# A convolution-and-MLP kernel: the first filter spectrum in 4 KB rows, the second half's sums in other tables, and a new order of all instructions

## The chip, the cores and the metric

The kernel runs on one core of a Trainium2 chip. The metric is the device time of one execution in microseconds; the text gives medians. The core has five engines that run their own instruction lists and wait for one another by semaphores: TensorE (PE in the profile; PEld is its weight load), VectorE (DVE), ScalarE (ACT), GpSimd (POOL) and SyncE (SP), which here issues transfers and computes nothing. Sixteen DMA engines move the data.

## The reference

Four steps follow each other on x, 2048 rows of 512 bf16 numbers: a long convolution, an MLP, and both again.

```python
x = A_q
x = x + _A_ref(_layernorm(x), A_k, A_v, A_shift_k, A_ssm_k, A_ssm_D)
x = x + _B_ref(_layernorm(x), B_w1, B_b1, B_w2, B_b2)
x = x + _A_ref(_layernorm(x), A_k, A_v, A_shift_k, A_ssm_k, A_ssm_D)
x = x + _B_ref(_layernorm(x), B_w1, B_b1, B_w2, B_b2)
```

`_A_ref(q, k, v, ...)` shifts k by a filter of four taps along the rows, multiplies by v to get kv, convolves kv along the 2048 rows with a filter of 2048 taps for each of the 512 channels (by a Fourier transform of length 4096), adds kv times ssm_D, and returns q times the result. `_B_ref` is a layer norm, a 512 to 1376 matmul with bias and GELU, and a 1376 to 512 matmul with bias. The filter, k and v are the same in both convolutions, so the convolved result y is the same and is computed once.

## The kernel before, in words

**The convolution.** The 2048 rows are two halves of 1024, and so is the filter. A transform of one of these four pieces is two stages of matmuls: `stage1` (L584) against a table of cosines and sines, and `stage2` (L596) against a table of twiddles, in eight tiles t = 0 to 7. Every tile of 128x1024 is evacuated from PSUM to SBUF by ScalarE (L480) or VectorE (L481). The tags in the code are h for the filter, x for k-times-v, 1 and 2 for the stages, `_0` and `_1` for the halves.

The spectrum of the first filter half, `h2_0`, lands in `HH` (R_4). For a complex product the real and imaginary parts, which sit on even and odd partitions, must be had the other way round as well. So an exchange, `swap`, copies `HH` into `HI` (R_5) with even and odd partitions exchanged, in eight DMA transfers of 256 KB: two by t (0 to 3, 4 to 7), two by half of the channels, two by parity. Each moves 64 partitions. In `HH` the 64 numbers of one t stand 512 apart from one channel group to the next, so a source row is eight runs of 256 numbers (512 bytes).

The first half's output needs `x2_0` times `h2_0`. VectorE multiplies 128x1024 pieces from `HH` and `HI` (L475, tag `x2_0`, sixteen instructions) into R_1 and R_2; `inverse1` (L701) and `inverse2` (L723) transform back into y. The second half's output needs two products: `x2_0` with the spectrum h2_0 plus h2_1 terms (formed by L795 in R_3, exchanged into R_HS1, multiplied in place as tag `p2`), and `x2_1` with `h2_0`, which is multiplied in place in `HH` and `HI`. The second product is added to the first (tag `sum`), the sum stands in `HH` and `HI`, and the second `inverse1` reads it there.

Stage 2's table for t = 0 to 3 is built on the chip: one piece of 1024 columns (`tab_s`) is loaded into R_C, and eight scaled copies of it are spread (L525 on ScalarE, L526 on VectorE or GpSimd). R_C lies at the start of W1's place, so W1's first piece may be loaded when all eight are done. The first L596 needs all eight.

**The MLP.** The rows go through as blocks, 128 rows per tile: tiles of 1, 1, 2, 2, 2 and then 2, 2, 2, 2 in the first half, 4, 4 and 4, 4 in the second. A block takes statistics (L836, L837, L841 to L851), a normalised copy (L861, L862), the product with y and the sum (L475), statistics and normalised copy again, and a transposed copy, by TensorE for the first two blocks (L913), by a DMA transpose from SyncE for the others (L905). Then 11 chunks of the first layer (L925, GELU by L930) and the second layer (L959, added to x by L963). The first layer needs all four pieces of W1 (344 KB each), the second layer W2 (five pieces of 256 KB and a last one with the bias).

**The order.** Nothing is scheduled when the kernel is built. A table `SEQ` lists all 1187 operations in the order in which they are given to the engines' lists, `ENGS` gives the engine where there is a choice, and `BANKS` the PSUM bank of each tile. Each engine then runs its list in order, so an instruction that waits holds up all that stand behind it. `sync` derives the waits from what each operation reads and writes, and waits never change the order. The numbers of `dma` such as 690.0 are the durations by which the waits of one instruction are sorted; they take no part in the order. The transfers stand in SyncE's list, apart from four that ScalarE issues. The second half's k is loaded by DMA transposes (L511) into the place that the h1_1 matmuls read, so these come after those matmuls.

Of the kernel before, what the change touches and what calls it, by code (L numbers as in the profile page):

```python
# [7 lines left out]
ALU = mybir.AluOpType  # L8
# [28 lines left out]
class Prog:  # L37
# [65 lines left out]
            "vvvvavapvaaavvvvvvappavva")  # L103
    BANKS = (
            "60134220040246260464023527646260464422641704406260402044222460264036206002442040460240044204402200242060"
            "02214460672065547427762753146306163013472457323653454722637670216234677756017404705647420335536736732725"
            "64012131754124707451256025141142451241256076713424307574243075601201643645720014030")

    def __init__(self, nc):
# [289 lines left out]
def bass_interleave_layers__ssm_conv_h3__mixer_channel_mlp__prompt_kernel(  # L399
        nc, A_q, A_k, A_v, A_shift_k, A_ssm_k, A_ssm_D, B_x, B_w1, B_b1, B_w2, B_b2, out):  # L400
    P = Prog(nc)
# [598 lines left out]
```

## Time and profile before

| what | value |
|---|---|
| runs | 234.78, 235.28, 236.21 us; median 235.28 |
| the profiled execution, its own time | 236.31 us |
| its span, first to last instruction | 234.4 us |
| granted TensorE clock | 1.000 |
| busy: TensorE, VectorE, ScalarE, GpSimd | 224.6, 179.1, 167.0, 57.4 us |
| exchanges and their landing | 16 transfers of 256 KB, median 4.0 us |
| first matmul of the first layer | 57.07 us after the span's start |

All times in the text count from the start of the span. "A <-B" behind a wait names the instruction that ended it, by the latest semaphore that the profile saw; a matmul's end is modelled, so TensorE counts as busy while matmuls overlap. In the chain a line with L is work of that line and "DMA out<-in" a transfer under way. `ar` is the one SBUF arena in which every buffer lies, `ps` is PSUM and `sm` the small float32 arena, so rows tell buffers apart by line and shape only. `tab_small` holds the identity, the stage-1 table and constants, `tab_s` the stage-2 table, `in_B_w` W1 or W2.

### The profile page before, as it was taken

The numbers are of one execution on the slowest core, as the hardware profiler recorded it, in microseconds if no ns is written. First come the engines' busy times: TensorE is split into PE (matmuls) and PEld (weight loads), VectorE is DVE, ScalarE is ACT, GpSimd is POOL, SyncE is SP. The second block draws the span as 40 slices with busy tenths as digits, with TensorE's granted clock in tenths as the row PEclk, the third lists the DMA queues.
The fourth block names the chain that finished last, engine by engine and source line by source line (L and its number), as shares of the span: only waits on it lengthen the run. The fifth ranks groups of instructions, "written<-read, shape, count | busy, mean of one in ns | idle before, by whom it ended". The sixth has DMA issues, their size and how long they took to land.

```text
span 234.4 us, 6524 instructions
## 1 busy us (share of the span) xinstructions
PE 224.6 (96%) x2765; PEld 147.3 (63%) x2765; DVE 179.1 (76%) x360; ACT 167.0 (71%) x262; POOL 57.4 (24%) x119
## 2 busy tenths in 40 slices
PE   5999899997999999999999999999999999999995
PEld 1898787965868597667866585744444444444452
DVE  0699989999999999999999997771777769413023
ACT  2778999998969689999969996896077335603710
POOL 1496000207302525335003521312011010300000
PEclk9999999999999999999999999999999999999999
DMA  6999479479638970022400214232200310042102
GB/s 182 377 369 313 165 219 283 101 223 192 154 69 253 144 105 3 1 48 48 134 4 3 45 25 106 54 134 45 46 0 3 67 22 0 8 84 93 41 14 79
DMA packets 40105, 24.93 MB, mean 106 GB/s; under 512 B 23590, under 2 KB 33676, under 8 KB 40076
## 3 DMA queue, kind: packets, MB, share of 16 engines
q1 hardware_dynamic: 39778, 24.36, 39.7%
q8 instruction: 22, 0.36, 0.6%
q10 hardware_dynamic: 298, 0.16, 0.3%
q14 instruction: 7, 0.06, 0.1%
HBM read 13.23 MB, written 2.10 MB: 65 GB/s over the span
## 4 chain that ended last, share of the span: by engine, by line
PE 82%; ACT 8%; DMA 5%; DVE 2%; SPq 1%; issue 1%; ACTq 0%
PE ps L925 32%; PE ps L959 30%; ACT ar L480 7%; PE ps L584 5%; PE ps L701 4%; DMA ar<-ar 3%; PE ps L596 3%; DMA ar<-tab_small 2%; DVE ar L475 2%; PE ps L641 2%; PE ps L567 2%; PE ps L723 1%; SPq L460 1%; PE ps L948 1%; PE ps L669 1%; PE ps L616 1%
## 5 line engine op out<-in xcount | busy, mean ns | idle before, releaser
L930 ACT ACTIVATE ar<-ps,sm 128x256 bf16<-128x256 f32 (+5 forms) x143 | 66.8, 526 | 41.0 <-PE ps L925 40.3
L925 PE MATMUL ps<-ar 128*128 128x256 bf16 (+5 forms) x572 | 81.9, 297 | 1.2 <-ACT ar L861 1.0
L959 PE MATMUL ps<-ar 128*128 128x512 bf16 (+1 forms) x341 | 78.7, 379 | 0.0
L480 ACT ACTIVATE ar<-ps 128x1024 bf16<-128x1024 f32 (+3 forms) x76 | 70.3, 1022 | 7.0 <-PE ps L584 4.6
L925 PEld LDWEIGHTS ps<-ar 128*128 128x128 bf16 (+1 forms) x572 | 52.8, 100 | 28.5 <-ACT ar L861 1.1
L475 DVE TENSOR_TENSOR ar<-ar 128x512 bf16<-128x512 bf16 (+3 forms) x105 | 63.5, 641 | 1.0 <-ACT ar L480 0.3
L959 PEld LDWEIGHTS ps<-ar 128*128 128x128 bf16 (+1 forms) x341 | 32.5, 98 | 35.5 <-DVE ar L952 0.2
L836 DVE BATCH_NORM_STATS2 sm<-ar 128x6 f32<-128x512 bf16 x64 | 42.7, 682 | 0.7 <-DMA ar<-in_A_q_dram 0.2
L963 DVE TENSOR_TENSOR ar<-ar,ps 128x512 bf16<-128x512 bf16 x31 | 20.9, 681 | 18.4 <-PE ps L959 18.3
L861 ACT ACTIVATE ar<-ar,sm 128x512 bf16<-128x512 bf16 x39 | 30.6, 812 | 3.3 <-DVE sm L848 1.9
L841 POOL TENSOR_SCALAR sm<-sm 128x2 f32<-128x2 f32 (+2 forms) x21 | 6.1, 293 | 100.3 <-DVE sm L837 100.0
L843 POOL TENSOR_TENSOR sm<-sm 128x2 f32<-128x2 f32 (+2 forms) x26 | 22.0, 848 | 33.6 <-DVE sm L841 31.8
L584 PE MATMUL ps<-ar 128*64 128x128 bf16 x512 | 18.4, 225 | 1.0 <-issue 0.4
L596 PE MATMUL ps<-ar 128*128 128x64 bf16 x512 | 18.3, 193 | 0.9 <-ACT ar L480 0.8
L596 PEld LDWEIGHTS ps<-ar 128*128 128x128 bf16 x512 | 16.8, 98 | 2.7 <-ACT ar L480 1.8
L584 PEld LDWEIGHTS ps<-ar 128*64 128x64 bf16 x512 | 15.5, 112 | 4.0 <-ACT ar L480 1.8
L851 POOL TENSOR_SCALAR sm<-sm 128x1 f32<-128x1 f32 x40 | 14.8, 387 | 1.8
L481 DVE CAST ar<-ps 128x1024 bf16<-128x1024 f32 (+1 forms) x11 | 12.7, 1169 | 2.0 <-PE ps L584 0.8
L862 DVE TENSOR_SCALAR ar<-ar,sm 128x512 bf16<-128x512 bf16 x25 | 9.9, 411 | 5.1 <-POOL sm L851 5.0
L701 PEld LDWEIGHTS ps<-ar 64*128 64x128 bf16 (+1 forms) x384 | 11.8, 114 | 1.8 <-issue 0.4
L701 PE MATMUL ps<-ar 64*128 64x64 bf16 (+1 forms) x384 | 12.4, 203 | 0.2 <-DVE ar L475 0.2
L837 DVE BATCH_NORM_AGGREGATE sm<-sm 128x2 f32<-128x6 f32 x64 | 10.7, 174 | 0.8
(45 smaller groups left out, 100.8 us busy)
## 6 DMA issues: line engine op xcount, KB each, us to landing
ar<-ar SPq DMA_DIRECT2D x16, 256.0 KB, 4.0
ar<-tab_s SPq DMA_DIRECT2D x9, 256.0 KB, 5.0
ar<-in_A_ssm_k_dram SPq DMA_DIRECT2D x8, 256.0 KB, 5.2
ar<-in_A_v_dram SPq DMA_DIRECT2D x8, 256.0 KB, 5.3
ar<-in_A_q_dram SPq DMA_DIRECT2D x8, 256.0 KB, 4.7
out_dram<-ar SPq DMA_DIRECT2D x7, 256.0 KB, 2.8
ar<-in_B_w_dram SPq DMA_DIRECT2D x4, 344.0 KB, 5.7
ar<-in_B_w_dram SPq DMA_DIRECT2D x5, 256.0 KB, 3.8
```

The lines of the kernel that those rows point to most:

```text
L475: return P.op(eng, lambda e: e.tensor_tensor(o, a, b, op), dur, reads=[a, b] + list(more), writes=[o])
L480: return e.activation(dst, src(), AF.Copy)
L584: r = e.matmul(Q(tl, 64 * ri, 64, i * 128, [1, 128]), w, m, start=True, stop=True)
L596: r = e.matmul(Q(tl, 0, 128, i // 8 * 512 + i % 8 * 4, [32, 16], [1, 4]), w, m, start=True, stop=True)
L701: r = e.matmul(Q(tl, 0, 128, i, *([32, 16], [1, 4]) if split else ([1, 128],)), w, m, start=n == 0, stop=n == 1)
L836: P.op(DVE, lambda e, sj=sj, x=x: e.bn_stats(sj, x), 600.0, reads=[x], writes=[sj])
L843: P.op(POOL, lambda e: e.tensor_tensor(r, v, hf, ALU.pow), 420.0 + 149.0 * n, reads=[v, hf], writes=[r])
L861: return e.activation(o, x, AF.Identity, bias=u, scale=r)
L925: r = e.matmul(Q(tl, 0, rows, 0, [1, w]), a, m, start=dk == 0, stop=dk == 3)
L930: P.op(ACT, lambda e, dst=dst, tl=tl, rows=rows, bias=bias, w=w: e.activation(dst, Q(tl, 0, rows, 0, [1, w]), AF.Gelu_apprx_tanh, bias=bia ...
L959: r = e.matmul(Q(tl, 0, 128, 0, [1, 512]), ins[fc][0], ins[fc][1], start=fc == 0, stop=fc == 10)
L963: P.op(DVE, lambda e, x=x, tl=tl: e.tensor_tensor(x, x, Q(tl, 0, 128, 0, [1, 512]), ALU.add), 604.0, reads=[x], writes=[x], tile=tl)
```

## The change

Three things change. The spectrum `h2_0` gets a layout in which all that one transfer takes of a partition is one run of 2048 numbers (4 KB): `run(t)` puts t = 0 to 3 in the first 4096 columns and 4 to 7 in the second, with 256 numbers per channel group. The exchange of `h2_0` is written out with these runs; the second exchange keeps `swap`. `hrun` replaces `hap` wherever `HH` or `HI` is read. The sums go into R_3 and R_HS1, whose layout the second `inverse1` needs, and it reads them there. And `SEQ`, `ENGS` and `BANKS` are new.

```diff
-        8, 1, 4, 3, 0, 25, 33, 5, 46, 2, 35, 36, 29, 37, 30, 38, 40, 56, 47, 26, 6, 57, 50, 58, 48, 49, 216, 9, 32,
...
+        46, 35, 44, 5, 0, 36, 25, 47, 8, 56, 1, 37, 6, 50, 3, 48, 2, 12, 216, 49, 61, 62, 9, 11, 57, 51, 58, 38, 52,
...
+    def run(t):
+        return 4096 * (t // 4) + 64 * (t % 4)
+
+    def hrun(t, d, g=None):
+        return A(0, 128, HH + run(t) + (2048 * g if g else 0), [d, 2], [256, 16 if g is None else 8], [1, 64])
...
-        evac(BOTH, A(0, 128, HH + 64 * t, [32, 2], [512, 16], [1, 32]),
+        dst = A(0, 128, HH + run(t), [32, 2], [256, 16], [1, 32])
+        evac(BOTH, dst,
...
-    swap(HH, HI)
+    for kh in range(2):
+        for c in range(2):
+            for g in range(2):
+                o = 4096 * kh + 2048 * c
+                src, dst = [PA(p, r + o, [1, 2048]) for p, r in ((g, HH), (1 - g, HI))]
+                dma(dst, src, 1 << 18, reads=[src])
...
-            tt(hap(R_1, t, R_2 - R_1, g), A(0, 128, HX + 1024 * t + 512 * g, [0, 2], [64, 8], [1, 64]), hap(HH, t, HI - HH, g), ALU.mult, 603.0)
+            spec = hrun(t, HI - HH, g)
+            tt(hap(R_1, t, R_2 - R_1, g), A(0, 128, HX + 1024 * t + 512 * g, [0, 2], [64, 8], [1, 64]), spec, ALU.mult, 603.0)
...
-            o, x = A(0, 128, R_3 + w, [512, 16], [1, 32]), A(0, 128, HI + w, [512, 16], [1, 32])
+            o = A(0, 128, R_3 + w, [512, 16], [1, 32])
+            x = A(0, 128, HI + run(t) + 32 * g, [256, 16], [1, 32])
...
-        o, p = hap(HH, t, HI - HH), hap(R_3, t, D1)
+        o, p = hrun(t, HI - HH), hap(R_3, t, D1)
         tt(o, A(0, 128, xo, [0, 2], [64, 16], [1, 64]), o, ALU.mult, 1137.0)
         P.tag = "sum"
-        tt(o, o, p, ALU.add, 1137.0)
+        tt(p, o, p, ALU.add, 1137.0)
     P.tag = "i1_1"
-    inverse1(HH, HI, R_Z1, True)
+    inverse1(R_3, R_HS1, R_Z1, range(8))
```

`inverse1` now takes the set of tiles that are split by partition halves instead of a flag: none in the first inverse and all eight in the second, as before. A function `inverse1_by_half` is added and not called. The number of instructions of each kind stays; 49 of the 1187 operations go to another engine. In the changed file line numbers from L701 on are higher: L701 becomes L708, L723 L749, L836 L870, L905 L939, L913 L947, L925 L959 and L959 L993.

Three places in the engines' lists matter below. The first is SyncE's list behind the first exchange. `128x1376` is a piece of W1, `128x2x512` two rows of tiles of W2, `DMA_TRANSPOSE` with `in_A_k` a part of the second half's k. Before, from the exchange's last two transfers on:

```order
23 L460 DMA ar<-ar 64x8x256 x2
24 L460 DMA ar<-in_B_b_dram 1x512
25 L470 DMA ar<-tab_small 128x1024
26 L460 DMA ar<-in_B_w_dram 128x1376
27 L460 DMA ar<-in_B_b_dram 128x10x1
28 L460 DMA ar<-in_B_w_dram 128x1376
29 L460 DMA ar<-in_B_b_dram 96x1
30 L460 DMA ar<-in_B_w_dram 128x2x512 x2
31 L470 DMA ar<-tab_small 128x1024
32 L460 DMA ar<-in_B_w_dram 128x2x512
33 L460 DMA ar<-in_A_v_dram 128x1024
34 L511 DMA_TRANSPOSE ar<-in_A_k_dram 128x4x128
```

Row 35 behind these holds the last two pieces of W1. Now, from the same point on (the first piece of W1 stands further ahead):

```order
26 L460 DMA ar<-ar 64x2048 x2
27 L460 DMA ar<-in_A_q_dram 128x1024
28 L460 DMA ar<-in_B_w_dram 128x2x512
29 L470 DMA ar<-tab_small 128x1024 x2
30 L460 DMA ar<-in_B_w_dram 128x1376 x2
31 L460 DMA ar<-in_B_w_dram 96x512
32 L460 DMA ar<-in_B_w_dram 128x1376
33 L460 DMA ar<-in_B_w_dram 128x2x512
34 L460 DMA ar<-in_A_v_dram 128x1024
35 L511 DMA_TRANSPOSE ar<-in_A_k_dram 128x4x128
36 L460 DMA ar<-in_B_w_dram 128x2x512
```

All of W1 has moved ahead of v and of the transposed k. Two further loads of v, two further transposes of k and then the last W2 pair follow row 36, so that pair stands behind three transposes; before, all five W2 pairs stood ahead of the first one.

The second place is the head of ScalarE's list: its own transfers, the spreads (L525) and the first evacuations (L480). Before:

```order
1 L460 DMA ar<-in_A_shift_k_dram 4x512
2 L494 ACT_TABLE_LOAD
3 L470 DMA ar<-tab_small 128x464
4 L460 DMA ar<-in_A_ssm_D_dram 1x512
5 L525 ACTIVATE ar<-ar,sm 128x64x16 x3
6 L480 ACTIVATE ar<-ps 128x1024 x3
7 L480 ACTIVATE ar<-ps 128x8x128
```

Now:

```order
1 L470 DMA ar<-tab_small 128x464
2 L460 DMA ar<-in_A_shift_k_dram 4x512
3 L494 ACT_TABLE_LOAD
4 L460 DMA ar<-in_A_ssm_D_dram 1x512
5 L480 ACTIVATE ar<-ps 128x1024 x4
6 L480 ACTIVATE ar<-ps 128x8x128 x2
7 L525 ACTIVATE ar<-ar,sm 128x64x16 x2
8 L480 ACTIVATE ar<-ps 128x1024 x4
```

The small table goes out first, and two spreads stand behind six evacuations where three stood ahead of all.

The third place is the head of SyncE's list. Before:

```order
1 L460 DMA ar<-in_A_ssm_k_dram 128x1024
2 L470 DMA ar<-tab_s 128x1024
3 L460 DMA ar<-in_A_ssm_k_dram 128x1024 x2
4 L460 DMA ar<-in_A_k_dram 128x1024 x4
5 L460 DMA ar<-in_A_ssm_k_dram 128x1024
```

Now:

```order
1 L460 DMA ar<-in_A_ssm_k_dram 128x1024 x3
2 L460 DMA ar<-in_A_k_dram 128x1024 x4
3 L470 DMA ar<-tab_s 128x1024
4 L460 DMA ar<-in_A_ssm_k_dram 128x1024
5 L460 DMA ar<-in_A_v_dram 128x1024 x4
```

The piece of the stage-2 table from which the spreads copy was the second transfer and is now the eighth.

More of the change, by code (lines that the diff above doesn't have):

```diff
@@ L44 @@
     SEQ = (
[55 rows of a table removed]
[55 rows of a table added]
     ENGS = (
[L101 to L103 removed]
+            "vpvpvaavvvpvpvpvpaaavaavaavaavaavavvapvpvaaavavaavavvaaaaaaaaaavaaaaaaaaaavvavaaaappppaaaaaaaaaaaaaaaaaa"
+            "aaaaaaaaaaappvvvvappvppaappvvppaappaappaappaappaappaappvappaappaappaappvappaavpavpvaavvvvvavappavvvvpvav"
+            "vvvvvvvpvavaapvvavvppvava")
     BANKS = (
[L105 to L107 removed]
+            "43425704240260260464026421646260464422651146066240462042042460264073240000242624060240240420420402002660"
+            "04675406756463017126444564377357251031642372632034153077467642440510216372656247321154646670057122342670"
+            "61221570264135541541572503434012067362744465151532307422176457027100036327547357472")
     def __init__(self, nc):
@@ L459, in dma @@
     def dma(dst, src, nbytes, reads=(), writes=None, eng=SP, paced=False):
-        o = P.op(eng, lambda e: e.dma_start(dst, src, allow_slow_non_contiguous=True), 690.0 if P.tag[:2] == "h2" else 475.0, reads=reads,
+        o = P.op(eng, lambda e: e.dma_start(dst, src, allow_slow_non_contiguous=True), 690.0 if P.tag == "h2_1" or P.tag == "h2_0" and not 1 else 475.0, reads=reads,
                     writes=[dst] if writes is None else writes, dma=True, nbytes=nbytes)
@@ L679, in shift_pair, with inverse1 @@
                 P.op(DVE, g, 604.0, reads=[v], writes=[o], tile=tl[h])
+    def run(t):
+        return 4096 * (t // 4) + 64 * (t % 4)
+    def hrun(t, d, g=None):
+        return A(0, 128, HH + run(t) + (2048 * g if g else 0), [d, 2], [256, 16 if g is None else 8], [1, 64])
     def hap(r, t, d, g=None):
         return A(0, 128, r + 64 * t + (4096 * g if g else 0), [d, 2], [512, 16 if g is None else 8], [1, 64])
-    def inverse1(p, q, Z, split):
+    def inverse1(p, q, Z, some):
         for j in range(8):
+            split = j in some
             tl = Tile(2)
@@ L709, in inverse1, with inverse1_by_half, f @@
                  lambda tl=tl: Q(tl, 0, 128, 0, [8, 16], [128, 8], [1, 8]), E1, tl)
+    def inverse1_by_half(p, q, Z):
+        for h in range(2):
+            for j in range(4):
+                tl = Tile(2)
+                ins = []
+                for i in range(16):
+                    dg = 16 * j + i
+                    for n, r in enumerate((p, q)):
+                        ins.append((i * 64, n, A(0, 128, r + (dg // 4) * 512 + dg % 4, [4, 128]), A(0, 128, R_U + n * 128 + 64 * h, [1, 64])))
+                def f(e, ins=ins, tl=tl):
+                    for i, n, w, m in ins:
+                        r = e.matmul(Q(tl, 0, 128, i, [1, 64]), w, m, start=n == 0, stop=n == 1)
+                    return r
+                P.op(PE, f, 32 * 32.0, reads=[x for y in ins for x in y[2:]], tile=tl)
+                evac(BOTH, A(0, 128, Z + 4096 * h + 128 * j, [512, 8], [8, 16], [1, 8]),
+                     lambda tl=tl: Q(tl, 0, 128, 0, [8, 8], [64, 16], [1, 8]), E1, tl)
     def inverse2(Z, YT):
@@ L782, in bass_interleave_layers__ssm_conv_h3__mixer_channel_mlp__prompt_kernel @@
     P.tag = "i1_0"
-    inverse1(R_1, R_2, R_3, 0)
+    inverse1(R_1, R_2, R_3, range(0, 8, 2) if 0 else ())
     P.tag = "i2_0"
```

4 lines of the change are left out of this document (1 added, 3 removed), and 108 rows, old and new, of the table SEQ.

## Prediction

> **What bounds the kernel now.** I read the page first, then busy time by stretch, then the chain of work that ended last, then the timelines around its joints.
>
> The page and three stretches of the span (microseconds, then busy time of each engine):
>
> ```profile
> PE 224.6 (96%) x2765; PEld 147.3 (63%) x2765; DVE 179.1 (76%) x360; ACT 167.0 (71%) x262; POOL 57.4 (24%) x119
> ```
> ```profile
> 25.00:57.00 32.00, 28.24 (x604) 23.40 (x600) 30.64 (x58) 30.53 (x35) 5.13 (x15) 1.00 0.75 191
> 57.00:125.00 68.00, 67.76 (x1024) 50.39 (x1026) 66.80 (x115) 59.15 (x115) 21.39 (x40) 1.00 0.41 86
> 125.00:232.00 107.00, 106.70 (x722) 55.48 (x714) 64.22 (x162) 60.19 (x96) 17.78 (x38) 1.00 0.19 46
> ```
>
> There are three regimes. From 57 us on TensorE stands still for 0.24 + 0.30 us in 175: its instructions are the same in both kernels, so that part can hardly shrink. From 25 to 57 VectorE and ScalarE are the full engines (30.6 and 30.5 of 32) and TensorE idles 3.76 us. From 57 to 125 VectorE is nearly full too (66.8 of 68). So a gain can come from an earlier start, from the stretch up to 57, or from a late input; it then stays to the end, if VectorE follows.
>
> The chain up to the first matmul of the MLP (start, length, what):
>
> ```profile
> 1.35 4.89 DMA ar<-tab_small
> ...
> 6.29 0.28 PE ps L547 x4
> ...
> 36.11 3.96 DMA ar<-ar
> ...
> 48.25 7.61 ACT ar L480 x9
> ...
> 57.07 0.84 PE ps L925 x12
> ```
>
> It starts at a table, passes the first exchange, the multiplications and the first inverse behind it and ScalarE's evacuations, and enters the MLP. Its last joint, which it gives to ScalarE, is wrong, as TensorE's timeline there shows:
>
> ```profile
> 54.73 0.40 PE L913 MATMUL ps<-ar 128*128 128x128 bf16 x4 [0.55 <-DVE sm L841]
> 54.96 1.10 PE L596 MATMUL ps<-ar 128*128 128x64 bf16 x32
> 57.07 0.84 PE L925 MATMUL ps<-ar 128*96 128x128 bf16 x12 [1.01 <-ACT ar L861]
> ```
>
> The matmul at 57.07 reads block 0's transposed rows, which the last of ScalarE's nine evacuations (48.25 + 7.61 = 55.86) delivers. L861, named as releaser, normalises block 1. The other input is W1. SyncE issued its last two pieces in this group (first row), and the DMA view of 51.15 to 51.60 holds the second of them alone (size, time to landing):
>
> ```profile
> 50.57 1.04 SPq L460 DMA_DIRECT2D ar<-in_B_w_dram  x2
> ```
> ```profile
> ar<-in_B_w_dram SPq DMA_DIRECT2D x1, 344.0 KB, 5.8
> ```
>
> It is issued at about 51.2 and lands at 51.2 + 5.8 = 57.0. The MLP waits 1.01 us for weights, not for ScalarE.
>
> **The change part by part.** *W1 sooner.* The last piece of W1 now stands ahead of all transposed loads of k, a few places behind the first exchange. The exchange's last transfer was issued at 36.11. Behind it SyncE has eight issues up to that piece, at about 0.5 us (two took 1.04): 36.1 + 4 + 5.8 = 46, and 54 were they three times as long. TensorE would then start when its L596 ends, at 56.06: **-1.01 us**.
>
> *The small table first.* ScalarE's issues and first work (issues carry a q):
>
> ```profile
> 0.74 0.55 ACTq L460 DMA_DIRECT2D ar<-in_A_shift_k_dram  x1
> 1.31 1.28 ACT L494 ACT_TABLE_LOAD   x1 [1.31 <-PEq L985]
> 1.35 0.36 ACTq L470 DMA_DIRECT2D ar<-tab_small  x1
> ...
> 6.47 3.23 ACT L525 ACTIVATE ar<-ar,sm 128x1024 bf16<-128x1024 bf16 x3 [3.87 <-DVE sm L518]
> 10.32 5.91 ACT L480 ACTIVATE ar<-ps 128x1024 bf16<-128x1024 f32 x6 [0.62 <-PE ps L584]
> 17.70 3.03 ACT L480 ACTIVATE ar<-ps 128x1024 bf16<-128x1024 f32 x3 [1.47 <-PE ps L584]
> ```
>
> The table is now issued at 0.74 instead of 1.35, 0.61 us sooner, and three pieces of the filter go out first on SyncE. TensorE begins with those transposes rather than with the taps. Bounds: 0 (the DMA engines were slow to start for other reasons) and 6.29 - 4.65 = 1.64 (the warm-up matmuls end there: 1.48 + 3.17).
>
> ```profile
> 1.48 3.17 PE L538 MATMUL ps<-ar 128*128 128x512 bf16 x7 [1.48 <-POOL ar L532]
> ```
>
> I take the issue's own shift, **-0.61 us**.
>
> *The spreads later.* The stage-2 table goes from SyncE's second issue to its eighth. Its eight copies ran on ScalarE (3.23 us for three) in the wait before 10.32; two now stand behind six evacuations, 2 x 1.08 = 2.15 us, where 1.47 us of waiting (the last row) covers most of it. VectorE takes four for three (0.88 us for two), GpSimd still two:
>
> ```profile
> 6.47 0.88 DVE L526 TENSOR_SCALAR ar<-ar,sm 128x1024 bf16<-128x1024 bf16 x2
> ```
> ```profile
> 13.32 5.79 POOL L526 TENSOR_SCALAR ar<-ar,sm 128x1024 bf16<-128x1024 bf16 x2
> ```
>
> Queued behind them are evacuations for which TensorE waits. Cost: 0 if those waits cover it, 2.15 - 1.47 = 0.68 on ScalarE if not; I take **0**, since VectorE's added copy (0.44) is paid by two statistics that it puts off. What a late table would do beyond that is a rival below.
>
> *The exchange in 4 KB rows.* Eight transfers keep their bytes; the source is one run per partition instead of eight. The nearest rows by size (count, size, us to landing):
>
> ```profile
> ar<-ar SPq DMA_DIRECT2D x16, 256.0 KB, 4.0
> ...
> out_dram<-ar SPq DMA_DIRECT2D x7, 256.0 KB, 2.8
> ```
> ```profile
> L475 DVE TENSOR_TENSOR ar<-ar 128x1024 bf16<-128x1024 bf16 x16 | 10.0, 685 | 0.1
> ```
>
> A store in 2 KB rows lands 1.2 us sooner. But the sixteen multiplications that read the exchange idled 0.1 us in all: VectorE was busy with the other multiplications while the rows travelled. **0**, between 0 and -0.1; with that cover gone it would be 1.2. The chain's step at 36.11 is a tie, not a stall. The Trainium skill, "DMA: Bandwidth & Descriptors", section "Why small descriptors are slow (HBM only)", speaks against this edit: copies from SBUF to SBUF do not pay for small pieces. By it the landing stays at 4.0 and the edit is worth 0 even without the cover; no run here shows the same copy in both forms yet.
>
> *The sums.* The same eight additions with another output; the inverse reads other columns with the same strides: **0**.
>
> *Order and waits after 57.* One stall there is on a transposed block:
>
> ```profile
> 103.90 0.61 PE L925 MATMUL ps<-ar 128*128 128x256 bf16 x4 [0.17 <-DMA ar<-ar]
> ```
>
> Block 5's first matmul has about 4 us more of TensorE's work ahead of it in the new order (the matmuls ahead in either order, at the durations of before): **-0.17**. One wait is added: W2's rows 2 and 3 now stand behind three transposed loads of k. One such load takes SyncE 1.3 us from 49.22; with one W2 piece and two of v ahead at 0.5 each the issue is near 49.2 + 3 x 1.3 + 3 x 0.5 = 54.6, and the landing 3.8 later at 58.4. The first second-layer matmul stood at 63.17, now about 61.5: **0**, with 3.1 us to spare.
>
> ```profile
> 49.22 1.30 SPq L511 DMA_TRANSPOSE ar<-in_A_k_dram  x1
> ```
> ```profile
> 63.17 1.73 PE ps L959 x8
> ```
> ```profile
> ar<-in_B_w_dram SPq DMA_DIRECT2D x5, 256.0 KB, 3.8
> ```
>
> **Sum:** 1.01 + 0.61 + 0.17 = 1.79 us off a span of 234.4, giving 232.6. That execution's own time was 236.31, the median of the runs 235.28; 235.28 - 1.8 = **233.5 us**.
>
> **The rivals.** *A: more comes free.* The table lands with the first filter piece, so the start gains the whole 1.64, and some of the other 3.76 - 1.01 = 2.75 us that TensorE idles between 25 and 57 goes too. For it: the first work waits for that one transfer. Against: the two engines that release TensorE there are full. 1.01 + 1.64 + 0.17 = 2.8 and up to 0.5 of the idle time: 235.28 - 3.1 = 232.2.
>
> *B: the gain stops at VectorE.* W1's microsecond is TensorE's alone. VectorE has 1.2 us of idle time in 57 to 125, and the sums must be done before the second inverse starts; a TensorE that comes early then waits there. For it: 66.8 of 68. Against: VectorE starts 0.61 sooner as well, and has slightly less to do ahead of the last sum. Only about 0.5 us would stay: 234.8.
>
> *C: slower, by late spreads.* The stage-2 table was second on SyncE; eighth, it lands about where a load of k did. All eight copies must be done before the first L596:
>
> ```profile
> 21.15 0.64 PE L596 MATMUL ps<-ar 128*128 128x64 bf16 x16
> ```
>
> If the last one, on GpSimd, ends late, every evacuation from 21 to 56 shifts with it. It decides against the change from 1.8 us of lateness on, which eats the whole sum. The most is the table's own delay. It was issued at 1.18 and landed 4.0 later, at 5.2; an eighth issue, seven times 0.5 after the first at 0.7, is at 4.2, and k's pieces, which stood there, took 5.4: 9.6, so 4.4 us.
>
> ```profile
> 1.18 0.41 SPq L470 DMA_DIRECT2D ar<-tab_s  x1
> ```
> ```profile
> ar<-tab_s SPq DMA_DIRECT2D x1, 256.0 KB, 4.0
> ```
> ```profile
> ar<-in_A_k_dram SPq DMA_DIRECT2D x4, 256.0 KB, 5.4
> ```
>
> Against: GpSimd's copies ran from 13.3 to 19.1 anyway, 2 us ahead of need. At 3 us of lateness: 235.28 + 3.0 - 1.8 = 236.5; at the most 237.9.
>
> *D: the change does not do what it says:* the rows get long but nothing waited for them. I hold this to be true, and it is in the sum as 0.
>
> **How the numbers follow.** One per cent, 2.35 us, is about what a measurement of this kernel can tell from no change; the edges are 232.9 and 237.6. The forecast has 0.50: it reaches from 232.4 to 234.6, so 0.13 of it is beyond the edge and 0.37 within. A has 0.19, all faster. B has 0.18, within. C has 0.13: 0.05 within, 0.08 slower. Together faster 0.32, same 0.60, slower 0.08. The range goes from 231.0 (A with another 1.2 us of the idle time) to 236.4 (about C's middle).
>
> **What would show it.** Right: the first real matmul near 5.7; the last piece of W1 landed before 50; the first MLP matmul near 55.5 with at most 0.2 us of idle time before it; no stall at block 5; and the multiplications of the first half idle no less than before though the exchange lands sooner. Wrong: a wait at the first L596 (C), new idle time of TensorE at the second inverse or at the transposed blocks (B), or a first MLP matmul still near 57.

## The result, and the profile after

| | before | changed |
|---|---|---|
| median of nine runs, on the same chip | 235.9 us (234.6 to 239.6) | 234.09 us (233.01 to 234.93) |
| profiled execution, own time and span | 236.31, 234.4 us | 234.05, 232.2 us |

Medians are over all executions; a ratio leaves out those more than 1.5% above the fastest of their kernel, and the profile of the run b_both below, which is such a one, is not used.

The ratio is 0.9932, 95% interval 0.9904 to 0.9959: 1.6 us faster, between 1.0 and 2.3. The medians differ by 1.8 us, the spans by 2.2; the profiled execution before was 0.4 us above its median, the changed one at its median, so about 0.4 of the 2.2 belongs to that one execution. The forecast was 233.5. Its mechanism for W1 held; its sizes for the start and its reason for the exchange did not.

TensorE's timeline at the start of the changed kernel (start, length, instruction; in brackets the idle time before it):

```profile
1.48 3.17 PE L538 MATMUL ps<-ar 128*128 128x512 bf16 x7 [1.48 <-POOL ar L532]
4.67 1.71 PE L567 MATMUL ps<-ar 128*128 128x128 bf16 x16
```

The transposes follow the warm-up matmuls without a pause; before, work began at 6.29 after 1.64 us of waiting. Matched operation by operation, the first stage-1 matmul is 2.0 us sooner and VectorE's first multiplication (L475, tag x2_0) 2.16: 30.61 against 32.77. From there half is lost in this execution. VectorE's timeline of those multiplications:

```profile
33.63 2.48 DVE L475 TENSOR_TENSOR ar<-ar 128x1024 bf16<-128x1024 bf16 x4
36.93 3.10 DVE L475 TENSOR_TENSOR ar<-ar 128x1024 bf16<-128x1024 bf16 x5 [0.82 <-DMA ar<-ar]
40.32 3.10 DVE L475 TENSOR_TENSOR ar<-ar 128x1024 bf16<-128x1024 bf16 x5 [0.30 <-DMA ar<-ar]
```

Two pauses, 1.12 us, both ended by a transfer of the exchange; before, there was 0.1. The group rows of 25 to 57 us say the same for VectorE and for the inverse behind it on TensorE (busy time, mean ns of one, idle time before them and its releaser):

```profile
L475 DVE TENSOR_TENSOR ar<-ar 128x1024 bf16<-128x1024 bf16 (+1 forms) x23 | 12.8, 604 | 1.1 <-DMA ar<-ar 1.1
...
L708 PE MATMUL ps<-ar 128*128 128x128 bf16 x128 | 7.5, 219 | 1.6 <-DVE ar L475 1.6
```

The first inverse is left 0.97 us sooner. The chain of work that ended last now runs through SyncE's issues and the exchange into the MLP:

```profile
31.52 2.29 SPq L460
34.99 5.31 DMA ar<-ar
40.32 3.11 DVE ar L475 x5
43.48 3.78 PE ps L708 x64
47.28 7.51 ACT ar L480 x9
54.84 1.07 PE ps L959 x16
```

At the joint to the MLP TensorE now stands 0.44 us and not 1.01, and for an evacuation. W1's last piece, alone in the DMA view of 40.1 to 40.7, took 6.4 us and landed at 46.6, 8 us ahead of need:

```profile
54.84 1.07 PE L959 MATMUL ps<-ar 128*128 128x128 bf16 x16 [0.44 <-ACT ar L480]
```
```profile
ar<-in_B_w_dram SPq DMA_DIRECT2D x1, 344.0 KB, 6.4
```

That matmul is 2.2 us sooner than before, the second inverse and the last blocks 2.14: hardly anything is won or lost after 55 us.

### The profile page after: what moved, and what is told of

It reads as the page before. It is cut to its first block, busy times and chain, and to the rows that moved or that the text cites. A ratio compares the mean times of both kernels' runs of the same rounds, so it can differ in the third digit from the quotient of the medians.

```text
span 232.2 us, 6497 instructions
## 1 busy us (share of the span) xinstructions
PE 221.7 (95%) x2743; PEld 146.6 (63%) x2765; DVE 180.3 (78%) x361; ACT 163.3 (70%) x258; POOL 59.9 (26%) x123
## 4 chain that ended last, share of the span: by engine, by line
PE 78%; ACT 7%; DMA 5%; SPq 4%; DVE 3%; issue 1%; DVEq 0%
PE ps L959 33%; PE ps L993 31%; ACT ar L480 7%; SPq L460 4%; PE ps L708 4%; PE ps L596 3%; DMA ar<-in_A_v_dram 3%; PE ps L584 3%; DMA ar<-ar 2%; PE ps L749 1%; DVE ar L475 1%; PE ps L982 1%; DVE ar L647 1%; PE ps L669 1%; PE ps L641 0%
## 5 line engine op out<-in xcount | busy, mean ns | idle before, releaser
L959 PE MATMUL ps<-ar 128*128 128x256 bf16 (+4 forms) x568 | 80.4, 297 | 0.7 <-ACT ar L480 0.4
L993 PE MATMUL ps<-ar 128*128 128x512 bf16 (+1 forms) x325 | 75.3, 379 | 1.5 <-issue 1.1
L480 ACT ACTIVATE ar<-ps 128x1024 bf16<-128x1024 f32 (+3 forms) x76 | 70.4, 1008 | 8.4 <-PE ps L584 5.7
L959 PEld LDWEIGHTS ps<-ar 128*128 128x128 bf16 (+1 forms) x572 | 52.9, 100 | 26.9 <-ACT ar L480 0.6
L475 DVE TENSOR_TENSOR ar<-ar 128x512 bf16<-128x512 bf16 (+2 forms) x104 | 63.1, 641 | 2.1 <-DMA ar<-ar 1.1
L993 PEld LDWEIGHTS ps<-ar 128*128 128x128 bf16 (+1 forms) x341 | 32.1, 98 | 35.4
L870 DVE BATCH_NORM_STATS2 sm<-ar 128x6 f32<-128x512 bf16 x64 | 42.7, 681 | 0.6
L877 POOL TENSOR_TENSOR sm<-sm 128x2 f32<-128x2 f32 (+2 forms) x26 | 21.4, 821 | 50.1 <-DVE sm L875 48.3
L895 ACT ACTIVATE ar<-ar,sm 128x512 bf16<-128x512 bf16 x36 | 28.0, 811 | 4.1 <-POOL sm L885 2.3
L875 POOL TENSOR_SCALAR sm<-sm 128x2 f32<-128x2 f32 (+2 forms) x21 | 4.5, 213 | 76.9 <-DVE sm L871 76.4
L596 PE MATMUL ps<-ar 128*128 128x64 bf16 x512 | 18.9, 193 | 0.3 <-ACT ar L480 0.3
L596 PEld LDWEIGHTS ps<-ar 128*128 128x128 bf16 x512 | 17.3, 98 | 2.6 <-ACT ar L480 0.7
L885 POOL TENSOR_SCALAR sm<-sm 128x1 f32<-128x1 f32 x43 | 18.1, 437 | 2.0
L896 DVE TENSOR_SCALAR ar<-ar,sm 128x512 bf16<-128x512 bf16 x28 | 11.1, 416 | 7.3 <-POOL sm L885 7.2
L708 PE MATMUL ps<-ar 64*128 64x64 bf16 (+1 forms) x384 | 12.3, 203 | 1.6 <-DVE ar L475 1.6
L708 PEld LDWEIGHTS ps<-ar 64*128 64x128 bf16 (+1 forms) x384 | 11.7, 114 | 3.2 <-DVE ar L475 1.9
L829 DVE SCALAR_TENSOR_TENSOR ar<-ar,sm,ps 128x512 bf16<-128x512 bf16 x16 | 11.0, 737 | 0.0
```

The costliest lines, as they stand in the source:

```text
L475: return P.op(eng, lambda e: e.tensor_tensor(o, a, b, op), dur, reads=[a, b] + list(more), writes=[o])
L480: return e.activation(dst, src(), AF.Copy)
L596: r = e.matmul(Q(tl, 0, 128, i // 8 * 512 + i % 8 * 4, [32, 16], [1, 4]), w, m, start=True, stop=True)
L708: r = e.matmul(Q(tl, 0, 128, i, *([32, 16], [1, 4]) if split else ([1, 128],)), w, m, start=n == 0, stop=n == 1)
L870: P.op(DVE, lambda e, sj=sj, x=x: e.bn_stats(sj, x), 600.0, reads=[x], writes=[sj])
L877: P.op(POOL, lambda e: e.tensor_tensor(r, v, hf, ALU.pow), 420.0 + 149.0 * n, reads=[v, hf], writes=[r])
```

## The experiments

The theory after the result: (1) the start gains 2 us, from the landings of the small table and of the filter pieces; (2) the exchange, queued on SyncE among other loads, gives 1 us of it back (so the changed kernel's profile); (3) W1 ahead of the transposed loads of k wins 1 us; (4) row length and sums win nothing. The rivals stand with each run. Every kernel was timed in five rounds beside the kernel before, whose medians in the three groups were 235.76, 235.95 and 235.75 us. Diffs that only move an instruction are shown as rows of an engine's list.

### u_rows: the changed kernel with 512-byte rows

```diff
-        return 4096 * (t // 4) + 64 * (t % 4)
+        return 64 * t
...
-                o = 4096 * kh + 2048 * c
-                src, dst = [PA(p, r + o, [1, 2048]) for p, r in ((g, HH), (1 - g, HI))]
+                o = 256 * kh + 4096 * c
+                src, dst = [PA(p, r + o, [512, 8], [1, 256]) for p, r in ((g, HH), (1 - g, HI))]
```

> The changed kernel with the first spectrum in the old layout again: each exchange transfer takes eight 512-byte runs per partition; the order and the sums stay changed. Theory T (the start came 1.9 us sooner, the exchange then became what VectorE waits for and took 1.1 us back, W1's early load gave 1.0): the exchange now counts, 512-byte pieces move fewer bytes per ns, so VectorE's waits of 0.8 and 0.3 us at the first multiplications grow by 0.3 to 0.8 us in all, span 232.5 to 233.0, ratio to before near 0.995. Rival R1 (the long rows are what the gain comes from): span back to about 234.4, ratio 1.000. Rival R2 (copies from SBUF to SBUF do not pay for small pieces): waits and span as in the changed kernel, 232.2, ratio 0.993.

Measured 234.15 us (232.84 to 235.78), ratio 0.995 (0.9919 to 0.998): the changed kernel's time, as the second rival had it. VectorE's waits did not grow (0.23 and 0.82 us). In its profile all stages are about 0.3 us later than in the changed kernel's, but 0.34 is there at the first stage-1 matmul, ahead of any exchange. In the new order the long rows are worth nothing that these runs can tell from 0, at most 0.3 us.

### x_sp: the changed kernel with four loads ahead of the exchange

On SyncE a bias piece, a W2 pair, a filter piece and a row tile of q stand among the exchange's transfers. They are moved ahead of it:

```diff
+ L460 DMA ar<-in_B_b_dram 96x1
+ L460 DMA ar<-in_B_w_dram 128x2x512
+ L460 DMA ar<-in_A_ssm_k_dram 128x1024
+ L460 DMA ar<-in_A_q_dram 128x1024
  L460 DMA ar<-ar 64x2048 x3
- L460 DMA ar<-in_B_b_dram 96x1
  L460 DMA ar<-ar 64x2048
- L460 DMA ar<-in_B_w_dram 128x2x512
- L460 DMA ar<-in_A_ssm_k_dram 128x1024
  L460 DMA ar<-ar 64x2048 x2
- L460 DMA ar<-in_A_q_dram 128x1024
  L460 DMA ar<-ar 64x2048 x2
```

> The changed kernel with four loads that stand between the exchange's transfers on SyncE (two of W2 and the bias, one filter piece, one q piece) moved ahead of all eight, into SyncE's idle time from 20 to 25 us. Theory T: the exchange's second half lands 1.3 us or more sooner, VectorE's waits of 0.82 and 0.30 us go, the first inverse starts up to 1.1 us sooner and that stays to the end: span near 231.1, ratio near 0.989. Rival (ScalarE, full from 20 to 55 us, holds the same stretch): the waits go, but the inverse or its evacuations start no sooner than 0.3 us earlier, span 231.9 to 232.2, ratio 0.992 to 0.993.

Measured 233.71 us (232.87 to 235.44), ratio 0.9939 (0.991 to 0.9969), span 231.1. VectorE's multiplications run through:

```profile
33.74 8.51 DVE L475 TENSOR_TENSOR ar<-ar 128x1024 bf16<-128x1024 bf16 x14
```

The last transfer landed at 35.58 instead of 40.30, the last multiplication ended 1.17 us sooner, and all behind it stayed 1.18 sooner to the end. So the theory's span came. Its ratio did not: 0.989 lies outside the interval, which holds the rival's 0.992 to 0.993. The profiled execution is the fastest of the twelve (232.87), and its first stage-1 matmul is 0.5 us sooner than the changed kernel's, ahead of any exchange. In the medians the gain over the changed kernel is 0.4 us and not certain.

Nor does the pause need this edit to vanish. u_w1 and u_w1b below have the changed kernel's queue up to the end of the exchange. Their last transfers landed at 38.50 and 39.75, and the multiplications paused 0 and 0.28 us. In u_w1:

```profile
34.27 8.51 DVE L475 TENSOR_TENSOR ar<-ar 128x1024 bf16<-128x1024 bf16 x14
```

With the same queue the last landing thus varies by 1.8 us, and the 1.12 us belong to the one execution that was profiled. What x_sp shows beyond that spread is the landing at 35.58; the last transfer was also issued 1.9 us sooner, at 33.11. And a lead can go elsewhere: in u_w1 and x_sp a stage-1 matmul near 26 us waits 1.15 and 0.93 us, 0.36 in the changed kernel. What that matmul waits for stays open.

### u_w1 and u_w1b: W1 late again

In u_w1 the last two pieces of W1 go behind the first transposed load of k; in u_w1b behind two transposed loads and three of v, as shown:

```diff
  L460 DMA ar<-in_A_v_dram 128x1024 x2
  L511 DMA_TRANSPOSE ar<-in_A_k_dram 128x4x128
+ L460 DMA ar<-in_B_w_dram 128x1376 x2
```

> The changed kernel with the last two pieces of W1 behind the first transposed load of k on SyncE, as they stood before. They should be issued near 49.6 and 50.1 and land near 55.5 to 56.3, where the first MLP matmul stands at 54.8. Theory T: TensorE waits 0.7 to 1.5 us there and all that follows shifts by it: span 232.9 to 233.7, ratio 0.996 to 1.000. Rival B of the prediction (VectorE sets the pace from 57 to 125): TensorE's wait is made up before the second inverse, span within 0.3 us of 232.2, ratio 0.993.

> The changed kernel with the last two pieces of W1 issued late again: behind two transposed loads of k and three loads of v, at about 51.5, so that they land near 56.3, where TensorE is ready for the first MLP matmul at 54.8. Theory (that matmul waits for W1 alone when W1 is late): TensorE stands from about 54.8 to 56.3, the rest of the kernel 1.5 us later, 234.1 + 1.5 = 235.6 in the median. Rival (the 1.0 us in the new order come from earlier evacuations, whatever W1 does): no change, 234.1.

u_w1: 233.85 us (233.03 to 234.33), ratio 0.9925 (0.9901 to 0.995). Its W1 landed at 53.75, 0.45 us ahead of the matmul at 54.20. The edit was too small to make W1 late, so it decides nothing on W1.

u_w1b: 238.49 us (238.18 to 238.89), ratio 1.0126 (1.0095 to 1.0157). The first MLP matmul waits for W1 in so many words:

```profile
57.27 1.07 PE L959 MATMUL ps<-ar 128*128 128x128 bf16 x16 [3.42 <-DMA ar<-in_B_w_dram]
```

It starts 2.43 us later than in the changed kernel. But all that follows is 4.04 later, more than either side expected. The other 1.6 us are TensorE's clock. In the windows behind the stall (length; busy time of PE, PEld, DVE, ACT, POOL; granted clock; DMA share; GB/s) it is 0.90, 0.50 and 0.75:

```profile
57.00:59.00 2.00, 1.73 (x28) 1.74 (x29) 1.17 (x3) 1.25 (x4) 1.39 (x4) 0.90 1.24 222
59.00:61.00 2.00, 2.00 (x22) 2.00 (x20) 0.00 (x0) 1.36 (x5) 0.00 (x0) 0.50 0.70 156
61.00:63.00 2.00, 2.00 (x42) 2.00 (x41) 0.53 (x1) 1.59 (x6) 0.00 (x0) 0.75 0.58 129
```

2 x (0.10 + 0.50 + 0.25) = 1.7 us of TensorE's work is lost there: one drop to 0.50, from 58.58 to 61.99.

### b_w1: the kernel before with W1 sooner

```diff
  L460 DMA ar<-in_B_w_dram 128x1376
+ L460 DMA ar<-in_B_w_dram 128x1376 x2
...
  L511 DMA_TRANSPOSE ar<-in_A_k_dram 128x4x128
- L460 DMA ar<-in_B_w_dram 128x1376 x2
```

> The kernel before with one edit: the last two pieces of W1 are issued right behind the second one, ahead of the W2 pairs, of v and of the first transposed load of k. Theory (W1 is the input for which the first MLP matmul waits, 1.01 us, and what is won there stays to the end): the last piece lands before 50, the first MLP matmul starts at about 56.1 instead of 57.07, all from there is 1.0 us sooner; 235.76 - 1.0 = 234.8 in the median. Rival 1 (ScalarE's evacuation or the first block's normalised rows release that matmul, as the profile's arrow says): no change, 235.8. Rival 2 (the gain stops at VectorE before the second inverse): the first MLP matmul is 1.0 sooner but the second inverse only about 0.5: 235.3.

Measured 235.11 us (234.66 to 238.28), ratio 0.9981 (0.9952 to 1.001): 0.8 us by the medians, which alone don't exclude 0. The profile shows the step. Up to the second stage of the inverse all is 0.52 us sooner than before (0.17 from an earlier landing of the small table, the rest gathered on the way); behind the joint it is 1.57. The 1.05 between is the stall, which is gone: L925 follows L596 at once.

```profile
54.44 1.10 PE L596 MATMUL ps<-ar 128*128 128x64 bf16 x32
55.39 0.87 PE L925 MATMUL ps<-ar 128*96 128x128 bf16 x12
```

0.4 us of it is given back at blocks 4 and 5, whose first matmuls then start within 0.1 us of their transposed rows. The second inverse is 1.16 us sooner, not the 0.5 of the rival by which VectorE stops the gain.

### u_head, u_act, u_sp: the changed kernel with the old start

u_act puts the taps' transfer and the activation table's load back ahead of the small table on ScalarE; u_sp makes the stage-2 table's piece SyncE's second transfer again; u_head does both. The first diff is ScalarE's list, the second SyncE's.

```diff
+ L460 DMA ar<-in_A_shift_k_dram 4x512
+ L494 ACT_TABLE_LOAD
  L470 DMA ar<-tab_small 128x464
- L460 DMA ar<-in_A_shift_k_dram 4x512
- L494 ACT_TABLE_LOAD
```
```diff
  L460 DMA ar<-in_A_ssm_k_dram 128x1024
+ L470 DMA ar<-tab_s 128x1024
  L460 DMA ar<-in_A_ssm_k_dram 128x1024 x2
  L460 DMA ar<-in_A_k_dram 128x1024 x4
- L470 DMA ar<-tab_s 128x1024
```

> The changed kernel with the old heads of two lists: ScalarE issues the small table behind the shift taps and its own table load, SyncE issues the stage-2 table second and the filter pieces in the old sequence. Theory T: the first filter transposes go back from 4.6 to about 6.5 us; the exchange's landing then no longer holds VectorE as much, so about 0.9 of the 1.9 us are seen at the end: span near 233.1, ratio near 0.997. Rival (the start carries through whole): span near 234.1, ratio 1.001. Rival (the exchange and ScalarE take all of it): span 232.2.

> The changed kernel with the old head of ScalarE's list alone: the taps' transfer and the table load of the activation function stand ahead of the small table again; SyncE's list is the changed one. Theory (the start is set by the later of two landings, the small table and the filter pieces, and the change moved both): the table is issued 0.6 us later and lands at about 5.7 instead of 4.54, the first transposes start at about 5.8 instead of 4.67, and what is left of this behind the exchange is 0.5 to 1.2 us: 234.6 to 235.3 in the median. Rival (the filter pieces alone set the start): the first transposes stay near 4.7, 234.1.

> The changed kernel with the old head of SyncE's list alone: the piece of the stage-2 table is the second transfer again, ahead of three filter pieces; ScalarE's list is the changed one. Theory (both landings count): the small table lands near 4.5 as now, the first filter piece sooner than now, but the second and third near 5.9 and 6.6 instead of 5.0 and 5.7; the first stage's matmuls lose 0.9 us, of which 0.4 to 0.9 are left behind the exchange: 234.5 to 235.0 in the median. Rival (the small table alone set the start, as the prediction had it): 234.1, with less waiting for the spreads.

| run | median, us | ratio, 95% | first transposes | last multiplication, against the changed kernel |
|---|---|---|---|---|
| u_head | 236.09 | 1.0025 (0.9991 to 1.0058) | 6.79 | +2.10 |
| u_act | 234.07 | 0.994 (0.9914 to 0.9966) | 5.08 | 0.00 |
| u_sp | 235.6 | 0.9995 (0.9962 to 1.0027) | 6.16 | +1.26 |

The small table first on ScalarE is worth nothing at the end; the expected 0.5 to 1.2 us did not come, nor did the rival's start near 4.7. In u_act the first transposes are 0.41 us later, the first stage-1 matmul 1.0 and the first multiplication 1.34 (more than the landing explains: TensorE's clock was still half there, as the last section shows), and then the pauses at the exchange vanish:

```profile
34.91 8.50 DVE L475 TENSOR_TENSOR ar<-ar 128x1024 bf16<-128x1024 bf16 x14
```

Fourteen multiplications in a row, the last of which ends when it did with two pauses. The last transfer landed at 40.24, against 40.30: in these two executions 1.3 us more or less of a head start changes nothing. The filter pieces' place is what counts. In u_sp they wait behind the table's piece:

```profile
6.16 1.92 PE L567 MATMUL ps<-ar 128*128 128x128 bf16 x16 [1.51 <-DMA ar<-in_A_ssm_k_dram]
```

The first transposes are 1.49 us later than in the changed kernel, the first stage-1 matmul 2.06 and the first multiplication 2.63; at the last one 1.26 stays. By the medians 1.5 us are lost, more than the 0.4 to 0.9 expected. u_head has both, and more: its TensorE stood 2.14 us ahead of the first transposes, and its clock was 0.84 from 6 to 9 us and 0.59 from 9 to 12, as behind the stall of u_w1b. A second drop, to 0.55 and 0.60 from 42 to 46, turns the 2.10 us into 3.7 by the end of the first inverse. Its ratio fits the rival by which the start carries through whole (1.001) and not the theory's 0.997. Why it lost that much stays open: the seven executions with a mean clock of at least 0.999 took 235.27 to 237.57 us, so these drops alone are not the reason.

### b_head and b_both: the new start in the old order

b_head moves, in the kernel before, the small table first on ScalarE and two filter pieces ahead of the stage-2 table's piece on SyncE. The spreads (L525, L526), which copy from that piece, stay at the head of ScalarE's and VectorE's lists. b_both adds the edit of b_w1.

```diff
  L460 DMA ar<-in_A_ssm_k_dram 128x1024
- L470 DMA ar<-tab_s 128x1024
  L460 DMA ar<-in_A_ssm_k_dram 128x1024 x2
+ L470 DMA ar<-tab_s 128x1024
```

> The kernel before with its start alone reordered: the small table is ScalarE's first transfer, and the three filter pieces stand ahead of the stage-2 table's piece on SyncE; old layout, old sums, W1 late as before. Theory (the start is set by the landings of table and pieces; part of it is given back at the exchange; W1's issue waits behind a transposed load that moves with the first stage's matmuls): the first transposes start near 4.7 instead of 6.5, about 1.0 us of that is left at the first inverse, and the first MLP matmul, still waiting for W1, starts near 56.1: 235.8 - 1.0 = 234.8 in the median. Rival (W1's landing at 57.0 does not depend on the start and swallows all): no change, 235.8.

> The kernel before with the two moves together and nothing else: the reordered start of the run above, and the last two pieces of W1 right behind the second one. Old layout of the spectrum, old sums, all else in the old order. Theory (these two moves are the whole of what the change gains): about 1.0 + 1.0 us, 233.8 in the median, as the changed kernel within 0.4 us. Rival (the long rows, the sums or the rest of the order bear a part): no better than 234.8.

Both expectations failed. b_head: 236.62 us (235.55 to 239.67), ratio 1.0034 (1.0002 to 1.0066), slower. b_both: 236.64 us (234.25 to 238.44), ratio 0.9995 (0.9953 to 1.0038), no gain. In b_both's four executions with a mean clock of 1.00 the time was 234.25 to 236.25 us, in the other four that count for the ratio 235.19 to 237.24. The start of b_head, on VectorE, ScalarE and TensorE:

```profile
7.96 0.88 DVE L526 TENSOR_SCALAR ar<-ar,sm 128x1024 bf16<-128x1024 bf16 x2 [3.07 <-DMA ar<-tab_s]
```
```profile
7.96 3.23 ACT L525 ACTIVATE ar<-ar,sm 128x1024 bf16<-128x1024 bf16 x3 [4.85 <-DMA ar<-tab_s]
```
```profile
4.83 0.26 PE L547 MATMUL ps<-ar 4*128 4x4 bf16 x4 [0.18 <-DMA ar<-tab_small]
5.02 2.43 PE L567 MATMUL ps<-ar 128*128 128x128 bf16 x24
10.19 4.05 PE L584 MATMUL ps<-ar 128*64 128x128 bf16 x80 [2.74 <-POOL ar L475]
```

TensorE starts 1.5 us sooner and then stands 2.74. The table's piece landed at 7.93 instead of 5.21; the spreads wait for it at the heads of two lists, and behind them the copies of the transposed filter, which stage 1 reads. Behind the stall the clock drops as well: the 80 stage-1 matmuls took 4.05 us, 2.94 before. The drop is not the whole reason: b_head's two executions with a mean clock of 1.00 took 236.49 and 236.83 us. So without the spreads' new place the new start does not pay; in the changed kernel, where they stand behind the first evacuations, it does. That their move alone would mend b_head is argued from these rows and was not run.

### b_rows: the long rows and the sums in the old order

The code is the changed kernel's; the order, the engines and the banks are those of before:

```diff
-        46, 35, 44, 5, 0, 36, 25, 47, 8, 56, 1, 37, 6, 50, 3, 48, 2, 12, 216, 49, 61, 62, 9, 11, 57, 51, 58, 38, 52,
...
+        8, 1, 4, 3, 0, 25, 33, 5, 46, 2, 35, 36, 29, 37, 30, 38, 40, 56, 47, 26, 6, 57, 50, 58, 48, 49, 216, 9, 32,
...
```

> The changed kernel's code (4 KB rows in the first exchange, sums in the other tables) with the old order, engines and PSUM banks of the kernel before. Theory (VectorE has other multiplications to do while the rows travel, and the sums cost the same anywhere): no change, 235.8 in the median, multiplications idle 0.1 us as before, though the exchange lands up to 0.3 us sooner per pair. Rival (shorter transfers shorten the path through the exchange): 0.5 to 1.2 us faster, 234.6 to 235.3.

Measured 234.7 us (234.13 to 236.55), ratio 0.9945 (0.9913 to 0.9976): 0.6 to 2.0 us faster, by the interval. The rival's number held, but not its path: the multiplications idle as little as before, and the first inverse gains nothing beyond what the start does. The step that is gone is the wait for W1. Before, SyncE stands 4.8 us at a bias piece that waits until another bias piece has landed, and only then come W2, v, the transposed k and W1 (the waits of SyncE's queue, then its timeline, of the kernel before):

```profile
SPq L460 <- DMA ar<-in_B_b_dram: 4.8, 1, 4.8
```
```profile
38.72 0.95 SPq L460 DMA_DIRECT2D ar<-in_B_w_dram  x1
44.47 0.33 SPq L460 DMA_DIRECT2D ar<-in_B_b_dram  x1
...
50.57 1.04 SPq L460 DMA_DIRECT2D ar<-in_B_w_dram  x2
```

And in b_rows:

```profile
38.01 0.87 SPq L460 DMA_DIRECT2D ar<-in_B_w_dram  x1
43.42 0.33 SPq L460 DMA_DIRECT2D ar<-in_B_b_dram  x1
...
49.69 1.04 SPq L460 DMA_DIRECT2D ar<-in_B_w_dram  x2
```

The bias piece, queued behind the exchange, lands 1.05 us sooner, W1's last piece at 55.51 instead of 56.98, and TensorE meets no wait at the MLP. The start of this execution was 0.54 us sooner by itself (the small table, issued at the same time, landed at 5.70 instead of 6.24), so the profile alone doesn't say how much of this the rows did. Nor are long rows needed for the sooner bias piece: in b_w1, with 512-byte rows, SyncE went on from the same wait at 43.52, 0.95 us sooner than before. The medians show that rows and sums together win about 1 us in the old order; how they do it is not shown. In the new order W1 has 8 us to spare, and the rows are worth nothing (u_rows).

### x_rows: x_sp with 512-byte rows

The diff is that of u_rows on top of x_sp's.

> The changed kernel with the four other loads ahead of the exchange (as in the run x_sp, 233.71), but with the old layout, 512-byte rows: the same copy in both forms with nothing queued in between. Theory (a 512-byte packet takes 27.5 ns and a 4 KB one 159 ns, so a transfer takes 0.88 instead of 0.64 us of each DMA engine; the multiplications that read the last transfer begin at 38.6): the last transfer lands near 36.3 instead of 35.6, and the time stays, 233.7. Rival (with no loads in between the long rows are what makes the exchange early): new idle time in the multiplications and 0.5 us or more slower, 234.2.

Measured 233.69 us (233.52 to 233.94), ratio 0.9897 (0.9854 to 0.9939), the time of x_sp. Fourteen multiplications run through again, now with 512-byte rows. The last transfer landed at 39.25, not near 36.3 and within the 38.50 to 40.30 of the changed kernel's queue, so moving the loads alone does not explain x_sp's 35.58; the multiplication that waits for it in the changed kernel starts here near 40.0, so 0.8 us of spare were left. The exchange's median time to landing in three pairs, 512-byte rows first and 4 KB rows second (before and b_rows; u_rows and the changed kernel; x_rows and x_sp):

```profile
ar<-ar SPq DMA_DIRECT2D x8, 256.0 KB, 3.9
```
```profile
ar<-ar SPq DMA_DIRECT2D x8, 256.0 KB, 3.4
```
```profile
ar<-ar SPq DMA_DIRECT2D x8, 256.0 KB, 4.0
```
```profile
ar<-ar SPq DMA_DIRECT2D x8, 256.0 KB, 4.0
```
```profile
ar<-ar SPq DMA_DIRECT2D x8, 256.0 KB, 3.4
```
```profile
ar<-ar SPq DMA_DIRECT2D x8, 256.0 KB, 3.0
```

The medians of the long rows are 0 to 0.5 us sooner, less than the eight transfers of one profile differ among themselves (2.4 to 4.5 us in x_sp, 2.7 to 5.4 in the changed kernel). The packets differ clearly: one of 512 bytes took 27 ns of a DMA engine, one of 4 KB 159, so 19 and 26 bytes per ns. The Trainium skill, "DMA: Bandwidth & Descriptors", section "Why small descriptors are slow (HBM only)", has it that such copies don't pay for small pieces. In the packets they do; in the landings these runs cannot tell.

## Why the prediction was near, point by point

- **W1 sooner, -1.01: right.** b_w1 wins 1.05 at that joint, 0.8 in the medians; u_w1b brings the wait back. That the profile named an activation as releaser there, and that it was wrong, is confirmed: moving W1 alone removed the wait.
- **Small table first, -0.61: wrong size and wrong cause.** The first transposes came 1.8 us sooner, close to rival A's whole 1.64, but u_act shows that the table's place is worth 0.4 there, 1.0 at the first stage-1 matmul and 0 at the end. The gain is the filter pieces' place ahead of the stage-2 table's piece, which the prediction mentioned and did not price: 1.26 us (u_sp's profile), 1.5 by the medians.
- **Spreads later, 0: right as a price, wrong as a step by itself.** Without it the earlier start wins nothing and costs 0.3% (b_head). Rival C's late table is real (it landed at 9.76, 9.6 forecast), but it hurts in b_head through the copies queued behind the spreads and not at the first L596; in the changed kernel nothing waits for it there.
- **Exchange in 4 KB rows, 0: right for the changed kernel, with a wrong reason.** The cover, VectorE's other multiplications, was assumed to stay. With a start 2 us sooner it did not, in the profiled execution: 1.12 us of pauses (0 and 0.28 in u_w1 and u_w1b). The prediction had the long rows worth 1.2 us in that case; u_rows shows 0 to 0.3. With the loads in between moved ahead there is no pause (x_sp, x_rows), but that wins no more than 0.4 us in the medians. In the old order rows and sums together do pay (b_rows), which the prediction did not see.
- **Sums, 0: not tried by themselves.** b_rows holds them together with the rows.
- **Block 5, -0.17: not seen.** The stall there is gone, as forecast, but the lead is 2.2 us at the first block and 2.14 at the second inverse, so nothing of it stayed.
- **W2 behind three transposes, 0: right.** The pair landed at 57.65; the first second-layer matmul started at 60.95.
- **Rival B did not come.** The second inverse starts 2.14 us sooner, as much as the MLP.

Of the signs named in advance, three came: W1's last piece before 50, no stall at block 5, the multiplications idle no less. Two did not: the first real matmul stood at 4.67 and not near 5.7, and the first MLP matmul idled 0.44 us and not at most 0.2.

The sum was 1.79 us against 1.8 in the medians and 2.2 in the spans, and that is partly luck. Two errors met: the start gained 1.2 to 1.5 us more than priced, and about 1.1 of it was lost again before the first inverse, where the prediction had priced nothing; in the changed kernel's profile it goes at the exchange, in u_w1's most of it near 26 us. W1's microsecond can be won only once: b_w1 and b_rows both end the same wait, and the changed kernel contains both. Open are the rows' share apart from the sums, the new place of the spreads tried alone, and how much of the start's gain is TensorE's clock (last section).

## What to carry to other kernels

Price an earlier start up to the next thing that does not move with it: here half of two microseconds was lost on the way, in one profile at the exchange's last landing, in another at a matmul ahead of it. Read such a loss in more than one execution before naming its cause. When an input is moved back in a queue, look for its readers at the heads of the engines' lists, since they hold up all behind them; such edits belong together. A load that waits for another load's landing stops every load behind it, and a weight far down that list then comes late for a reason the matmul's row doesn't name.

## What the runs showed of the hardware

A stall of TensorE can cost more than its length. Behind stalls of 2.14 us (u_head), 2.74 (b_head) and 3.42 (u_w1b) the granted clock was 0.50 for 3.41 us (from 8.06, 10.28 and 58.58), which takes 1.7 us of work. The window of u_head:

```profile
8.06:11.47 3.41, 3.41 (x58) 3.22 (x56) 1.53 (x4) 1.24 (x2) 2.15 (x5) 0.50 1.05 403
```

Behind 1.01 us (before, at 57.07) and 1.38 (changed, at 39.48) no drop is seen; the changed kernel's trace has no record of the clock, but the 64 inverse matmuls behind that stall took 3.76 us, and 3.83 and 3.76 before. A stall's length does not decide alone: u_head's second drop, 3.41 us from 42.19, came behind one of 1.04 us with three of 0.2 to 0.3 just before it, and the changed kernel had 1.38 with 0.28 and 0.20 before it. In the 3.41 us ahead of the four drops TensorE was busy for 0.67 to 1.88 us, but also for 1.73 in u_w1b from 51.76, where none followed. The rule stays open. In ten of b_head's twelve runs the mean clock is 0.993, which one such drop in 235 us gives (1.7 / 235 = 0.7%). The Trainium skill, "TensorE: Matmul & The Clock Gate", section "HAM oscillation — how this bites in real kernels", puts the limit at gaps above about 3.4 us; these runs show drops behind shorter ones.

The kernels also begin at half the clock. The trace records the clock only from a later moment on, and the views count the time before it as 1.00. In the kernel before that moment is 10.34, and the stage-1 matmuls took 308 ns each just ahead of it and 220 behind it (groups of 9.3 to 10.3 and of 10.5 to 12 us):

```profile
L584 PE MATMUL ps<-ar 128*64 128x128 bf16 x22 | 1.3, 308 | 0.0
```
```profile
L584 PE MATMUL ps<-ar 128*64 128x128 bf16 x60 | 1.9, 220 | 0.0
```

From one start to the next these are 53 and 28 ns. In the changed kernel, without a record, the transposes are slow up to about 6.0 (310 ns each, then 232). The full clock came at 9.2 to 10.8 us in before, b_w1, b_rows, u_sp and u_act, at 4.2 to 7.4 in u_rows, x_sp, x_rows, u_w1 and u_w1b, and in u_head at 4.64, to drop again at 8.06. So a part of what the start gains or loses in a single profile is this moment; no run tried it apart.

The landing of one transfer varies between executions with the same issue: the small table, issued at 1.35, landed at 6.24, 6.06 and 5.70 in three profiles of the old start. That moves a whole execution by half a microsecond, so single profiles of these kernels differ by that much for no reason of theirs.
